# Decoding and splitting each weight tile once, with both parts kept in DRAM, in a fused attention and two-layer block on one core

## The chip, the cores and the metric

One core of a Trainium2 chip runs the whole program as one launch. The metric is the device time of that launch in microseconds. The kernel before takes 1089.96 us, the median of three runs (1089.48 to 1090.23).

## The reference

The inputs are float32 for attention and float64 for the weights of the two feed-forward layers (`moe_*`, `moe2_*`). Attention has 4 batches, 8 heads, 576 positions, head size 64; its bias comes from a small network on the relative position.

```python
scores = q @ k.T / 8 + bias(|i - j|, i)          # (4, 8, 576, 576)
attn   = exp(scores - rowmax) ; attn /= sum + 1e-9
x      = (attn @ v) as (2304, 512)               # tokens x model
h      = max(max(x @ w1, x @ w2), x @ w3)        # 512 -> 768
x      = h @ w_out                               # 768 -> 512
g      = elu(x @ w_in)                           # 512 -> 2048
out    = g @ w_out2                              # 2048 -> 512
```

## The kernel before

**Precision.** Each matrix product of the feed-forward layers is done with operands split into a high part `hi`, rounded to the matmul type fp32r, and a rest `lo = x - hi`. Three matmuls (hi·hi, hi·lo, lo·hi) replace one. The weights come as float64 bit patterns, so a tile of [128, 512] weights arrives as `raw`, [128, 512, 2] int32. The generator `decoder` (L350) turns it into float32 with five VectorE instructions (DVE: L358, L361, L363, L365, L368) and one ScalarE instruction (ACT: L360). Each `yield` ends a piece; `pump(k)` runs k pieces, so calls of `pump` spread the decoding over the program. Piece four also calls `fetch`, which issues the load of the tile after next.

**Weights.** There are 56 tiles: 18 for the first layer (`w1`: 6 column blocks m times 3 matrices w), 6 of its output matrix (`wo`), and 32 of the second layer (`wi` and `w3`, 16 each). The decoded float32 tiles stay in SBUF (`t10`, `T1`, `t2a`, `t2b`), except `wo`, which passes through DRAM (`scw`).

**Stages.** Everything is written out by hand (`manual_schedule`); engines run their instructions in program order.

1. The bias tables (L138 to L197) are computed and stored in DRAM.
2. Attention is a software pipeline of 80 steps, 5 for each of 16 head pairs and batches. `plan` holds (key, function) pairs; a step s puts its operations at keys s + `OFF`. At key s + 0.30 and 0.31 DVE computes the scores with the bias, at 0.32 comes one `pump` (59 of the 80 steps), then ACT evacuates the transposes of step s - 2 (`evac`, 0.36 to 0.39) and takes exponentials (`expo`, 0.38 and 0.40), with `norm` of step s - 1 on GpSimd (POOL) and DVE at 0.34 and 0.35. `lim` lets 9 tiles (3 `w1`, 6 `wo`) be decoded here.
3. The first layer goes over three token blocks th of 768 tokens. For each of the 18 tiles, `moe1_mm` runs 24 matmuls into one of 4 pairs of PSUM banks and `moe1_ev` takes the maximum (ACT for w = 0, DVE for w = 1, 2) and splits the result (ACT `hh`, POOL `hl`). `split_w1`, two tiles ahead, splits the float32 tile into hi and lo on POOL, and does so again for each th. In th = 0, `pump(3)` stands ahead of each evacuation: the other 15 `w1` tiles are decoded there. `moe1_out` multiplies by the output matrix (8 groups of 18 matmuls); for th = 0 and 1 it comes after the first column block of the next th.
4. The second layer goes over three token blocks blk and 16 blocks f: `moe2_g` (24 matmuls, then ELU and split) and `moe2_out` (18 matmuls of 512 columns). `split_w2` splits two tiles for each of the 48 (blk, f) on POOL. For blk = 0 `pump(5)` stands in each half of `moe2_g`, between two ACT instructions and ahead of the DVE instruction that frees the PSUM bank.

All DMAs are issued on SyncE (SP), in program order, each after the semaphores it waits for.

Of the kernel before, what the change touches and what calls it, by code (L numbers as in the profile page):

```python
# [10 lines left out]
F32 = mybir.dt.float32  # L11
# [15 lines left out]
NB = 384  # L27
# [21 lines left out]
def fused_kernel(ctx, tc, tkq, vv, lt, pk, wm1, wo1, win2, wo2, out):  # L49
# [3 lines left out]
    const = ctx.enter_context(tc.tile_pool(name="const", bufs=1))  # L53
    wpre = ctx.enter_context(tc.tile_pool(name="wpre", bufs=1))
    dram = ctx.enter_context(tc.tile_pool(name="dram", bufs=1, space=DRAM))

# [4 lines left out]

    scw = [dram.tile([128, 512], F32, name=f"scw{kk}") for kk in range(NM1)]
    scr = [dram.tile([128 if c < 4 else 64, H, S], F32, name=f"scr{c}") for c in range(5)]
# [9 lines left out]
    def lo_of(eng, dst, src, hi):  # L73
        e = nc.gpsimd if eng == "p" else nc.vector
        e.tensor_tensor(out=dst, in0=src, in1=hi.bitcast(F32), op=ALU.subtract)  # L75
# [173 lines left out]
    def trans0(s):  # L249
        n, c = steps[s]  # L250
        for k in range(4):
            nc.tensor.transpose(T0[:, 128 * k:128 * k + 128], E[s][:, 128 * k:128 * k + 128], ident)  # L252
        if c == 0:
            PT[n, 0] = [wpre.tile([128, 4, 256], F32, tag="big", name="p0", bufs=3) for _ in range(2)]
        elif c == 2:
            PT[n, 1] = [tp.tile([128, 4, 320], F32, tag=f"p{h}", name="p1", bufs=1) for h in range(2)]
        if c in (0, 2):
            PT[n, c // 2].append(tp.tile([128, 256], F32, tag="p3", name="p3", bufs=3))
        elif c == 4:
            PT[n, 1].append(tp.tile([64, 128], F32, tag="p4", name="p4", bufs=1))  # L260
# [65 lines left out]
    for m in range(NM1):  # L326
        DQ += [("w1", m, w) for w in range(3)]
        if m == 0:
            DQ += [("wo", kk, 0) for kk in range(NM1)]
    for f in range(NF):  # L330
        DQ += [("wi", f, 0), ("w3", f, 0)]
    RAW, TW = {}, {}
    n_raw = [0]
# [11 lines left out]

    dst_of = {}
    lim = [3 + NM1]

    def decoder():
        for i, key in enumerate(DQ):  # L350
            while i >= lim[0]:
                yield
            dst = dst_of[key[0]](key)
            t = dst.bitcast(I32)
# [13 lines left out]
            nc.vector.tensor_tensor(out=t, in0=t, in1=x, op=ALU.bitwise_or)  # L368
            TW[key] = dst
            yield  # L370
            if key[0] == "wo":
                yield
                nc.sync.dma_start(scw[key[1]], dst)
                yield

    def load_wo(kk):
        t = wpre.tile([128, 512], F32, tag="to", name="to", bufs=2)
        nc.sync.dma_start(t, scw[kk])
        return t

    def split_wo(kk, t):
        hi_of("a", WO["h"][:, kk, :], t)
        lo_of("p", WO["l"][:, kk, :], t, WO["h"][:, kk, :])

    dec = decoder()
    WO = {}

# [4 lines left out]
    def need(key):  # L392
        while key not in TW:
            next(dec)

    WS = {}

    def split_w1(th, m, w):
        hi, lo = wpre.tile([128, 2, 512], F32R, tag="big", name="whl", bufs=3).rearrange("p j n -> j p n")
        need(("w1", m, w))  # L400
        t = TW["w1", m, w]
        hi_of("p", hi, t)
        lo_of("p", lo, t, hi)
        WS[th, m, w] = (hi, lo)

    dst_of["w1"] = lambda key: t10[key[2]] if key[1] == 0 else T1[key[1] - 1][key[2]]
    dst_of["wo"] = lambda key: wpre.tile([128, 512], F32, tag="to", name="to", bufs=2)
    t10 = [wpre.tile([128, 512], F32, name=f"t10_{w}") for w in range(3)]

# [9 lines left out]
    def moe1_mm(th, m, w):  # L419
        hi, lo = WS.pop((th, m, w))  # L420
        ps = PS[th, m, w] = pair()
# [9 lines left out]
    def moe1_ev(th, m, w):  # L431
        ps = PS.pop((th, m, w))
        for blk in range(2):
            p = ps[blk][:, 0:NB]
            if th == 0 or (th == 1 and m == 0):
                pump(3)
            if w == 0:
# [48 lines left out]
    at(3.05, fetch)  # L486
    at(MOE_AT["s0"], split_w1, 0, 0, 0)
    at(MOE_AT["s1"], split_w1, 0, 0, 1)
    at(MOE_AT["mm"], moe1_mm, 0, 0, 0)
# [7 lines left out]

    lim[0] = 4 * NM1
    seq = [(blk, f) for blk in range(3) for f in range(NF)]

    W2 = {}

    def split_w2(nm, i):
        if i >= len(seq):
            return
        blk, f = seq[i]
        hi = ws.tile([128, 512], F32R, tag="h" + nm, name="h" + nm)
        lo = ws.tile([128, 512], F32R, tag="l" + nm, name="l" + nm)
        need((nm, f, 0))
        t = TW[nm, f, 0]  # L510
        hi_of("p", hi, t)
        lo_of("p", lo, t, hi)
        W2[nm, blk, f] = (hi, lo)


    with ExitStack() as m1:
        wop = m1.enter_context(tc.tile_pool(name="wop", bufs=1))
        hp_ = m1.enter_context(tc.tile_pool(name="hp", bufs=NM1 + 1))
        t1s = ExitStack()
        t1p = t1s.enter_context(tc.tile_pool(name="t1p", bufs=1, side="right"))  # L520

        WOH = WO["h"] = wop.tile([128, NM1, 512], F32R, name="woh")
        WOL = WO["l"] = wop.tile([128, NM1, 512], F32R, name="wol")
        T1 = [[t1p.tile([128, 512], F32, name=f"t1_{m}_{w}") for w in range(3)] for m in range(1, NM1)]
        def moe1_out(th):
            for m in range(NM2):
                ps = pair()
                ms = slice(128 * m, 128 * m + 128)
                for blk in range(2):
                    bs = slice(blk * NB, blk * NB + NB)  # L530
                    j = 0
                    for kk in range(NM1):
                        HH, HL = HT[th, kk]
                        for wt, xt in ((WOH, HH), (WOH, HL), (WOL, HH)):
                            mm(ps[blk][:, 0:NB], wt[:, kk, ms], xt[:, bs], start=(j == 0), stop=(j == 3 * NM1 - 1))  # L535
                            j += 1
                for blk in range(2):
# [4 lines left out]
                    nc.vector.tensor_tensor(out=xl, in0=p, in1=xh.bitcast(F32), op=ALU.subtract)  # L542
                    yield

        with tc.manual_schedule():
            order = [(th, m, w) for th in range(3) for m in range(NM1) for w in range(3)]
            for i, (th, m, w) in enumerate(order):
                if w == 0:
                    HT[th, m] = (hp_.tile([128, TB], F32R, tag="hh", name="hh"), hp_.tile([128, TB], F32R, tag="hl", name="hl"))
                if i + 2 < len(order):  # L550
                    split_w1(*order[i + 2])
                if th == 0 and m and w == 0:
                    wo_t = load_wo(m - 1), load_wo(m) if m == NM1 - 1 else None
                if th == 0 and m and w == 2:
                    split_wo(m - 1, wo_t[0])
                    if wo_t[1]:
                        split_wo(m, wo_t[1])
                if i:
                    moe1_mm(th, m, w)
                    moe1_ev(th, m, w)  # L560
                if m == 0 and w == 2 and th > 0:
                    for _ in moe1_out(th - 1):
                        pass
            t1s.close()
            t2a = ctx.enter_context(tc.tile_pool(name="t2a", bufs=1, side="right"))

            ws = ctx.enter_context(tc.tile_pool(name="ws", bufs=2, side="right"))
            dst_of["wi"] = dst_of["w3"] = lambda key: (t2a if key[1] < 3 else t2b).tile([128, 512], F32, name=f"t2_{key[0]}{key[1]}")
            lim[0] += 6
            for i, _ in enumerate(moe1_out(2)):  # L570
                pump(3)
                if i == 4:
                    split_w2("wi", 0)
                if i == 6:
                    split_w2("w3", 0)
                    split_w2("wi", 1)
            lim[0] = len(DQ)


    t2b = ctx.enter_context(tc.tile_pool(name="t2b", bufs=1))  # L580
    mp = ctx.enter_context(tc.tile_pool(name="mp2", bufs=2))
    GT = {}

    def moe2_g(blk, f):
        hi, lo = W2.pop(("wi", blk, f))
        GH = mp.tile([128, TB], F32R, tag="gh", name="gh")
        GL = mp.tile([128, TB], F32R, tag="gl", name="gl")
        GT[blk, f] = (GH, GL)
        for q in range(2):
# [9 lines left out]
            nc.scalar.activation(t, p, AF.Relu, scale=-1.0)  # L599
            if blk == 0 and f > 0:  # L600
                pump(5)
            nc.scalar.activation(t, t, AF.Exp, scale=-1.0)
# [5 lines left out]
    def moe2_out(blk, f, acc):  # L608
        hi, lo = W2.pop(("w3", blk, f))
        GH, GL = GT.pop((blk, f))  # L610
# [5 lines left out]
    with tc.manual_schedule():  # L616
        moe2_g(0, 0)
        for i, (blk, f) in enumerate(seq):
            split_w2("wi", i + 2)
            split_w2("w3", i + 1)  # L620
            if i + 1 < len(seq):
# [4 lines left out]
            if f == NF - 1:  # L626
                for t in range(6):
                    if t % 2 == 0:
                        o = wpre.tile([128, 2, 512], F32, tag="big", name="o_t", bufs=3)
                    r0 = blk * TB + 128 * t  # L630
# [70 lines left out]
```

## Time and profile before

| | us |
|---|---|
| median of three runs | 1089.96 |
| the profiled execution | 1089.01 |
| its span on the core | 1087.2 |
| PE (TensorE matmul) busy | 1036.8 |
| DVE busy | 564.3 |
| ACT busy | 489.7 |
| POOL busy | 534.0 |

Busy time is from the profiled execution. PE matmuls overlap, and their ends are modelled, so PE's busy time is an upper estimate; what limits a stage is read from the stage.

### The profile page before, as it was taken

What the parts mean: (1) busy time and instruction counts of PE and PEld (TensorE: products, weight loads), DVE (VectorE), ACT (ScalarE), POOL (GpSimd) and SP (SyncE); (2) the same over time, 40 slices, a digit from 0 to 9 for tenths busy, and PEclk for the clock granted to TensorE, in tenths of its full rate; (3) what the DMA queues carried; (4) which work ended last, traced back from release to release, by engine and by line L of the source; (5) the groups of instructions that cost most, each with busy time, mean ns of one, the idle gap of its engine ahead of it and who ended that gap; (6) DMA issues with size and microseconds to landing.
All of it is one profiled execution on the core that took longest, in us unless ns stands there. A gap on an engine that the chain in (4) does not pass through costs nothing.

```text
span 1087.2 us, 16728 instructions
## 1 busy us (share of the span) xinstructions
PE 1036.8 (95%) x6200; PEld 867.0 (80%) x6200; DVE 564.3 (52%) x1172; ACT 489.7 (45%) x1075; POOL 534.0 (49%) x541
## 2 busy tenths in 40 slices
PE   7999999999999869999999999878899999999998
PEld 4456666666668769999999998767789999999997
DVE  7977777777775991111111159999952111121111
ACT  8978788778872231111111124333334333343332
POOL 0022332323235557245605425767686677667663
PEclk9999999999999898999999999999999999999999
DMA  7733435243222330000000013333301000010001
GB/s 270 276 113 130 144 107 172 93 134 130 98 64 69 107 122 34 1 1 1 1 1 1 1 59 96 110 98 104 97 20 59 1 1 1 1 60 1 1 1 59
DMA packets 30674, 77.04 MB, mean 71 GB/s; under 512 B 5504, under 2 KB 6400, under 8 KB 30592
## 3 DMA queue, kind: packets, MB, share of 16 engines
q1 hardware_dynamic: 30592, 75.95, 21.1%
q8 instruction: 50, 0.82, 0.3%
q14 instruction: 32, 0.26, 0.1%
HBM read 59.03 MB, written 16.91 MB: 70 GB/s over the span
## 4 chain that ended last, share of the span: by engine, by line
PE 78%; DVE 16%; issue 3%; ACT 1%; POOL 1%; DMA 0%; DVEq 0%; SPq 0%; ACTq 0%; POOLq 0%
PE bk L596 13%; PE pb L614 9%; PE pb L428 8%; PE bk L428 8%; PE pb L219 7%; PE bk L294 7%; PE bk L614 4%; PE bk L252 4%; PE bk L535 3%; PE pb L535 3%; PE pb L181 2%; PE bk L264 2%; PE pbb L181 2%; DVE t_w L363 2%; DVE t_wi L361 2%
## 5 line engine op out<-in xcount | busy, mean ns | idle before, releaser
L245 POOL TENSOR_SCALAR e_t<-e_t,st_t 128x576 f32<-128x576 f32 x64 | 66.0, 1031 | 233.4 <-DVE st_t L239 215.2
L603 DVE SCALAR_TENSOR_TENSOR t_t<-t_t,bk 128x384 f32<-128x384 f32 x96 | 52.9, 551 | 233.1 <-POOL lw L75 169.0
L75 POOL TENSOR_TENSOR gl<-t_t,gh 128x384 fp32r<-128x384 f32 x96 | 100.8, 1050 | 125.7 <-ACT gh L69 125.3
L596 PE MATMUL bk<-xh,hwi 128*128 128x384 f32 x384 | 132.4, 345 | 21.4 <-DVE t_t L603 21.4
L228 DVE CUSTOM_DVE_ANT_0 e_t<-pb,b_t 128x576 f32<-128x576 f32 x144 | 104.0, 756 | 56.3 <-PE pb L219 35.8
L596 PE MATMUL bk<-xh,lwi 128*128 128x384 f32 x384 | 131.2, 342 | 0.0
L596 PE MATMUL bk<-xl,hwi 128*128 128x384 f32 x384 | 130.8, 341 | 0.0
L428 PE MATMUL pb<-xh,whl 128*128 128x384 f32 x448 | 119.5, 343 | 6.0 <-POOL whl L67 4.0
L69 ACT ACTIVATE p<-bk 128x512 f32<-128x512 f32 (+2 forms) x224 | 99.1, 473 | 53.9 <-PE bk L252 53.7
L428 PE MATMUL bk<-xh,whl 128*128 128x384 f32 x416 | 111.1, 343 | 8.5 <-POOL whl L67 7.0
L233 ACT ACTIVATE e_t<-e_t,st_t 128x576 f32<-128x576 f32 x144 | 111.8, 777 | 2.5 <-DVE st_t L228 2.5
L69 ACT ACTIVATE gh<-t_t 128x384 fp32r<-128x384 f32 x96 | 50.4, 525 | 138.0 <-DVE t_t L603 138.0
L599 ACT ACTIVATE t_t<-bk 128x384 f32<-128x384 f32 x96 | 46.1, 480 | 122.5 <-PE bk L596 122.5
L596 PEld LDWEIGHTS bk<-xh,hwi 128*128 128x128 f32 x384 | 73.4, 191 | 28.1 <-DVE t_t L603 25.6
L428 PEld LDWEIGHTS pb<-xh,whl 128*128 128x128 f32 x448 | 83.0, 192 | 7.4 <-POOL whl L67 4.3
L428 PEld LDWEIGHTS bk<-xh,whl 128*128 128x128 f32 x416 | 77.2, 193 | 9.9 <-POOL whl L67 7.6
L219 PE MATMUL pb<-kq_t 64*128 64x288 f32 x512 | 80.7, 429 | 1.3 <-DVE st_t L228 1.3
L294 PE MATMUL bk<-p,tv_t 128*64 128x320 f32 (+1 forms) x512 | 76.0, 418 | 0.5 <-ACT xf L315 0.5
L428 PE MATMUL pb<-xl,whl 128*128 128x384 f32 x224 | 76.4, 341 | 0.0
L614 PE MATMUL pb<-hw,gh 128*128 128x512 f32 x192 | 76.1, 397 | 0.0
L614 PE MATMUL pb<-lw,gh 128*128 128x512 f32 x192 | 76.0, 396 | 0.0
L69 ACT ACTIVATE hh<-a_t 128x384 fp32r<-128x384 f32 x36 | 18.5, 525 | 125.7 <-DVE a_t L441 125.6
(116 smaller groups left out, 2347.4 us busy)
## 6 DMA issues: line engine op xcount, KB each, us to landing
raw<-wo SPq DMA_DIRECT2D x22, 512.0 KB, 3.6
scr<-o_t SPq DMA_DIRECT2D x36, 288.0 KB, 3.6
kq_t<-tkq SPq DMA_DIRECT2D x16, 640.0 KB, 4.8
raw<-wm SPq DMA_DIRECT2D x18, 512.0 KB, 3.6
raw<-win SPq DMA_DIRECT2D x16, 512.0 KB, 3.6
tv_t<-vv SPq DMA_DIRECT2D x16, 384.0 KB, 3.4
b_t<-scr SPq DMA_DIRECT2D x16, 288.0 KB, 4.2
b_t<-scr SPq DMA_DIRECT2D x16, 256.0 KB, 4.0
```

The lines of the kernel that those rows point to most:

```text
L69: nc.scalar.activation(dst, src, AF.Copy)
L75: e.tensor_tensor(out=dst, in0=src, in1=hi.bitcast(F32), op=ALU.subtract)
L219: mm(PB[h][:, o], t[r, 640 + 128 * c:768 + 128 * c], t[r, k0:k0 + 288], start=True, stop=True)
L228: nc.vector.tensor_tensor_reduce(out=E[s][:, 576 * h:576 * h + 576], in0=PB[h][:, 224:800], in1=BT[n // 4, c, h], op0=ALU.add, op1=ALU.min ...
L233: nc.scalar.activation(e, e, AF.Exp, bias=st[:, h:h + 1], scale=-1.0, accum_out=st[:, 2 + h:3 + h])
L245: nc.gpsimd.tensor_scalar(e, e, r, 1.0, op0=ALU.mult, op1=ALU.mult)
L294: mm(XO[64 * h:64 * h + 64, 0:w], v[:, 128 * k + 64 * h:128 * k + 64 * h + 64], ps[h][:, k, :], start=(k == 0), stop=False, skip_group_che ...
L428: mm(ps[blk][:, 0:NB], wt[:, ks], xt[:, kk, t0:t0 + NB], start=(j == 0), stop=(j == 11))
L535: mm(ps[blk][:, 0:NB], wt[:, kk, ms], xt[:, bs], start=(j == 0), stop=(j == 3 * NM1 - 1))
L596: mm(p, wt[:, ks], xt[:, kk, t0:t0 + NB], start=(j == 0), stop=(j == 11))
L603: nc.vector.scalar_tensor_tensor(out=t, in0=t, scalar=-1.0, in1=p, op0=ALU.add, op1=ALU.max)
L614: mm(acc[t], g[:, ts], w, start=(f == 0 and j == 0), stop=(f == NF - 1 and j == 2))
```

## The change

All 56 tiles go through one stream, in the order `w1`, `wo`, then `wi` and `w3`. After the five decoding instructions the decoder itself splits the tile: ACT copies it into the high half of a new tile `sp2`, POOL subtracts into the low half, and one later piece issues a store of both halves (512 KB) to DRAM (`SCW`), one tile late. Each use loads both halves back into a ring of six buffers `wr`, four to five uses ahead. The splits on POOL at each use are gone, as are the resident float32 tiles. During attention 12 tiles may be decoded; in the first layer `pump(2)` stands ahead of each evacuation in all three token blocks, and `pump(3)` after each evacuation of `moe1_out`; the second layer has no `pump`.

```diff
+    wr = ctx.enter_context(tc.tile_pool(name="wr", bufs=6))
@@ DQ (order of tiles), lim
     for m in range(NM1):
         DQ += [("w1", m, w) for w in range(3)]
-        if m == 0:
-            DQ += [("wo", kk, 0) for kk in range(NM1)]
+    DQ += [("wo", kk, 0) for kk in range(NM1)]
-    lim = [3 + NM1]
+    lim = [12]
@@ decoder
-            dst = dst_of[key[0]](key)
+            dst = wpre.tile([128, 512], F32, tag="t", name="t_w", bufs=2)
...
             nc.vector.tensor_tensor(out=t, in0=t, in1=x, op=ALU.bitwise_or)
-            TW[key] = dst
+            sp2 = wpre.tile([128, 2, 512], F32R, tag="sp2", name="sp2", bufs=2)
+            hi_of("a", sp2[:, 0], dst)
+            lo_of("p", sp2[:, 1], dst, sp2[:, 0])
+            todo.append((key, sp2))
             yield
-            if key[0] == "wo":
-                yield
-                nc.sync.dma_start(scw[key[1]], dst)
-                yield
+            if len(todo) > 1:
+                store()
+    def store():
+        key, sp2 = todo.pop(0)
+        d = dram.tile([128, 2, 512], F32, name=f"scw_{key[0]}_{key[1]}_{key[2]}")
+        nc.sync.dma_start(d, sp2.bitcast(F32))
+        SCW[key] = d
+    def load_w(key):
+        need(key)
+        t = wr.tile([128, 2, 512], F32R, tag="w", name="w_t")
+        nc.sync.dma_start(t.bitcast(F32), SCW[key])
+        WS.append((key, t))
@@ moe1_ev
-            if th == 0 or (th == 1 and m == 0):
-                pump(3)
+            pump(2)
@@ moe1_out, after each evacuation
-                    yield
+                    pump(3)
@@ loop of the first layer
-                if i + 2 < len(order):
-                    split_w1(*order[i + 2])
+                load_w(nxt[i + 4])
...
+                if th == 0 and m == NM1 - 1:
+                    load_wo(2 * w)
+                    load_wo(2 * w + 1)
@@ moe2_g
-            if blk == 0 and f > 0:
-                pump(5)
@@ loop of the second layer
-            split_w2("wi", i + 2)
-            split_w2("w3", i + 1)
+            for key in load2[2 * i + 4:2 * i + 6]:
+                load_w(key)
```

## Rows read from the trace of the kernel before

**Rows 1.** Windows: stretch, length, busy (x instructions) of five engines, PEclk, DMA share, GB/s.
```profile
58.00:317.00 259.00, 258.10 (x1792) 162.68 (x1792) 198.79 (x610) 208.97 (x539) 76.74 (x92) 1.00 0.37 121
334.59:439.74 105.15, 91.19 (x482) 88.76 (x482) 71.73 (x94) 24.00 (x44) 66.30 (x60) 0.92 0.26 86
651.98:796.17 144.19, 122.77 (x582) 108.11 (x582) 138.91 (x169) 54.46 (x113) 95.70 (x79) 0.96 0.33 99
796.17:1082.40 286.23, 286.23 (x1434) 259.97 (x1434) 48.22 (x82) 106.84 (x216) 196.87 (x203) 0.99 0.04 13
```

**Rows 2.** Chain of work that ended last: start us, us, what.
```profile
334.59 4.38 PE pb L428 x24
...
439.74 6.26 PE pb L535 x36
...
464.72 4.16 PE pb L428 x24
...
717.30 1.45 DVE t_wi L361
...
727.87 1.45 DVE t_wi L361
...
845.74 4.19 PE bk L596 x24
...
854.05 4.19 PE bk L596 x24
```

**Rows 3.** Waits, 334 to 440 us and 652 to 796 us: total, times, longest.
```profile
PE bk L428 <- POOL whl L67: 7.0, 2, 5.4
...
PE bk L596 <- DVE t_t L603: 19.4, 12, 2.4
```

**Rows 4.** One line's instructions (ns min/median/max): two in attention, one 340 to 408.
```profile
L358 DVE TENSOR_SCALAR x_t<-raw x11: 418/425/449, 78.2 to 324.8; 128x512 int32<-128x512 int32 x11
...
L363 DVE SCALAR_TENSOR_TENSOR to<-raw,to x6: 689/702/707, 148.7 to 295.8; 128x512 int32<-128x512 int32 x6
...
L441 DVE TENSOR_TENSOR a_t<-bk,a_t x8: 545/549/553, 344.4 to 402.8; 128x384 f32<-128x384 f32 x8
```

**Rows 5.** Groups by line, 685.6 to 780.7 us: busy us, mean ns, idle before.
```profile
L361 DVE TENSOR_SCALAR t_wi<-raw 128x512 int32<-128x512 int32 x10 | 15.2, 1520 | 0.0
...
L603 DVE SCALAR_TENSOR_TENSOR t_t<-t_t,bk 128x384 f32<-128x384 f32 x18 | 9.8, 544 | 0.0
```

**Rows 6.** One line's instructions on POOL, 465 to 540 us.
```profile
L67 POOL TENSOR_SCALAR whl<-t x17: 618/619/627, 469.0 to 535.5; 128x512 fp32r<-128x512 f32 x17
...
L75 POOL TENSOR_TENSOR whl<-t,whl x17: 1289/1306/1308, 469.7 to 536.2; 128x512 fp32r<-128x512 f32 x17
L75 POOL TENSOR_TENSOR hl<-a_t,hh x11: 1013/1017/1020, 476.4 to 538.8; 128x384 fp32r<-128x384 f32 x11
```

**Rows 7.** Timeline of two attention steps: start us, us, engine, line, operation.
```profile
200.76 0.72 ACT L360 ACTIVATE x_t<-x_t,rebias 128x512 int32<-128x512 int32 x1
...
214.85 0.77 ACT L69 ACTIVATE p<-bk 128x512 f32<-128x512 f32 x2 [0.77 <-PE bk L252]
...
215.62 0.69 DVE L368 TENSOR_TENSOR to<-to,x_t 128x512 int32<-128x512 int32 x1
...
216.26 0.60 ACT L69 ACTIVATE p<-bk 128x512 f32<-128x512 f32 x1
...
216.78 0.97 POOL L245 TENSOR_SCALAR e_t<-e_t,st_t 128x576 f32<-128x576 f32 x1 [2.29 <-DVE st_t L239]
...
218.14 0.60 PE L264 MATMUL bk<-ident,e_t 128*128 128x128 f32 x4
```

**Rows 8.** Groups by line, whole span, ACT's copy of a 128x512 tile.
```profile
L69 ACT ACTIVATE woh<-to 128x512 fp32r<-128x512 f32 x6 | 3.6, 621 | 0.1
```

**Rows 9.** Windows, columns as in Rows 1: the busiest stretch of the DMA queue.
```profile
27.20:54.40 27.20, 27.20 (x333) 12.39 (x324) 27.20 (x65) 26.41 (x39) 0.00 (x0) 1.00 0.76 276
```

**Rows 10.** DMA issues: tile, count, KB each, median us to landing.
```profile
raw<-wm SPq DMA_DIRECT2D x18, 512.0 KB, 3.6
...
out<-o_t SPq DMA_DIRECT2D x15, 256.0 KB, 2.5
scw<-to SPq DMA_DIRECT2D x6, 256.0 KB, 4.3
```

More of the change, by code (lines that the diff above doesn't have):

```diff
@@ L60, in fused_kernel @@
     nc.vector.memset(rebias, -896.0 * 2.0 ** 23)
-    scw = [dram.tile([128, 512], F32, name=f"scw{kk}") for kk in range(NM1)]
     scr = [dram.tile([128 if c < 4 else 64, H, S], F32, name=f"scr{c}") for c in range(5)]
@@ L253, in trans0 @@
         if c == 0:
-            PT[n, 0] = [wpre.tile([128, 4, 256], F32, tag="big", name="p0", bufs=3) for _ in range(2)]
+            PT[n, 0] = [tp.tile([128, 4, 256], F32, tag="pa", name="p0", bufs=3) for _ in range(2)]
         elif c == 2:
@@ L327, in fused_kernel @@
         DQ += [("w1", m, w) for w in range(3)]
-        if m == 0:
-            DQ += [("wo", kk, 0) for kk in range(NM1)]
+    DQ += [("wo", kk, 0) for kk in range(NM1)]
     for f in range(NF):
         DQ += [("wi", f, 0), ("w3", f, 0)]
-    RAW, TW = {}, {}
+    RAW = {}
     n_raw = [0]
@@ L344, in fetch @@
         RAW[key] = r
-    dst_of = {}
-    lim = [3 + NM1]
+    lim = [12]
+    SCW = {}
     def decoder():
@@ L368, in decoder @@
             nc.vector.tensor_tensor(out=t, in0=t, in1=x, op=ALU.bitwise_or)
-            TW[key] = dst
+            sp2 = wpre.tile([128, 2, 512], F32R, tag="sp2", name="sp2", bufs=2)
+            hi_of("a", sp2[:, 0], dst)
+            lo_of("p", sp2[:, 1], dst, sp2[:, 0])
+            todo.append((key, sp2))
             yield
-            if key[0] == "wo":
-                yield
-                nc.sync.dma_start(scw[key[1]], dst)
-                yield
-    def load_wo(kk):
[L377 to L383, printed above, removed]
+            if len(todo) > 1:
+                store()
+        while todo:
+            store()
+    todo = []
+    def store():
[3 more added lines that the diff above has]
+        SCW[key] = d
+    def load_wo(kk):
+        need(("wo", kk, 0))
+        nc.sync.dma_start(WO[:, kk].bitcast(F32), SCW["wo", kk, 0])
     dec = decoder()
-    WO = {}
     def pump(k=1):
@@ L392, in need, with take_w @@
     def need(key):
[L393 to L408, printed above, removed]
+        while key not in SCW:
+            if all(k != key for k, _ in todo):
+                next(dec)
+            else:
+                store()
+    WS = []
+    def load_w(key):
[3 more added lines that the diff above has]
+        WS.append((key, t))
+    def take_w(key):
+        k, t = WS.pop(0)
+        assert k == key
+        return t[:, 0], t[:, 1]
     TB = 2 * NB
@@ L419, in moe1_mm @@
     def moe1_mm(th, m, w):
-        hi, lo = WS.pop((th, m, w))
+        hi, lo = take_w(("w1", m, w))
         ps = PS[th, m, w] = pair()
@@ L486, in fused_kernel @@
     at(3.05, fetch)
-    at(MOE_AT["s0"], split_w1, 0, 0, 0)
-    at(MOE_AT["s1"], split_w1, 0, 0, 1)
+    for i in range(4):
+        at(MOE_AT["s0"], load_w, ("w1", i // 3, i % 3))
     at(MOE_AT["mm"], moe1_mm, 0, 0, 0)
@@ L495, in fused_kernel @@
     att.close()
-    lim[0] = 4 * NM1
     seq = [(blk, f) for blk in range(3) for f in range(NF)]
[L501 to L513, printed above, removed]
+    load2 = [("wi", 0, 0)]
+    for i, (blk, f) in enumerate(seq):
+        load2 += [("wi", s[1], 0) for s in seq[i + 1:i + 2]] + [("w3", f, 0)]
+    lim[0] = len(DQ)
     with ExitStack() as m1:
@@ L518, in fused_kernel @@
         hp_ = m1.enter_context(tc.tile_pool(name="hp", bufs=NM1 + 1))
[L519 to L524, printed above, removed]
+        WO = wop.tile([128, NM1, 2, 512], F32R, name="wo_t")
         def moe1_out(th):
@@ L533, in moe1_out @@
                         HH, HL = HT[th, kk]
-                        for wt, xt in ((WOH, HH), (WOH, HL), (WOL, HH)):
-                            mm(ps[blk][:, 0:NB], wt[:, kk, ms], xt[:, bs], start=(j == 0), stop=(j == 3 * NM1 - 1))
+                        for wt, xt in ((0, HH), (0, HL), (1, HH)):
+                            mm(ps[blk][:, 0:NB], WO[:, kk, wt, ms], xt[:, bs], start=(j == 0), stop=(j == 3 * NM1 - 1))
                             j += 1
@@ L542, in moe1_out @@
                     nc.vector.tensor_tensor(out=xl, in0=p, in1=xh.bitcast(F32), op=ALU.subtract)
-                    yield
+                    pump(3)
         with tc.manual_schedule():
             order = [(th, m, w) for th in range(3) for m in range(NM1) for w in range(3)]
+            nxt = [("w1", m, w) for th, m, w in order] + load2[:4]
             for i, (th, m, w) in enumerate(order):
@@ L549, in fused_kernel @@
                     HT[th, m] = (hp_.tile([128, TB], F32R, tag="hh", name="hh"), hp_.tile([128, TB], F32R, tag="hl", name="hl"))
-                if i + 2 < len(order):
-                    split_w1(*order[i + 2])
[L552 to L557, printed above, removed]
+                load_w(nxt[i + 4])
                 if i:
@@ L560, in fused_kernel @@
                     moe1_ev(th, m, w)
+                if th == 0 and m == NM1 - 1:
+                    load_wo(2 * w)
+                    load_wo(2 * w + 1)
                 if m == 0 and w == 2 and th > 0:
[L562 to L580, printed above, removed]
+                    moe1_out(th - 1)
+            moe1_out(2)
     mp = ctx.enter_context(tc.tile_pool(name="mp2", bufs=2))
@@ L584, in moe2_g @@
     def moe2_g(blk, f):
-        hi, lo = W2.pop(("wi", blk, f))
+        hi, lo = take_w(("wi", f, 0))
         GH = mp.tile([128, TB], F32R, tag="gh", name="gh")
@@ L608, in moe2_out @@
     def moe2_out(blk, f, acc):
-        hi, lo = W2.pop(("w3", blk, f))
+        hi, lo = take_w(("w3", f, 0))
         GH, GL = GT.pop((blk, f))
@@ L628, in fused_kernel @@
                     if t % 2 == 0:
-                        o = wpre.tile([128, 2, 512], F32, tag="big", name="o_t", bufs=3)
+                        o = mp.tile([128, 2, 512], F32, tag="o", name="o_t", bufs=3)
                     r0 = blk * TB + 128 * t
```

## The prediction

> **What bounds the kernel now.** First the windows by stage. In attention PE is busy 258.10 of 259.00 us, DVE 198.79 and ACT 208.97 [rows 1]: PE sets the pace, and the other two have about a fifth of the time free. In the first token block of the first layer the picture turns: PE 91.19 of 105.15 us. In the first token block of the second layer PE has 122.77 of 144.19 and DVE 138.91; in the rest of that layer PE is never idle [rows 1].
>
> Next the chain of waits, for the length of one unit of work. A step of the first layer (24 matmuls) is 4.16 us and one `moe1_out` is 464.72 - 439.74 = 24.98 us. A step of the second layer, where PE is full, is 854.05 - 845.74 = 8.31 us; in its first token block it is 727.87 - 717.30 = 10.57 us, and the chain there runs through DVE's decoding instructions [rows 2].
>
> From these the two losses:
> - First layer: from 334.59 to 439.74 lie 20 steps. 105.15 - 20 x 4.16 = 21.9 us lost. The other two token blocks show none.
> - Second layer: from 651.98 to 1082.40 lie 48 steps. 430.4 - 48 x 8.31 = 31.5 us lost, all in the first token block.
>
> Last the waits: PE waits for the split on POOL in the one, for the DVE instruction that frees the bank in the other [rows 3]. That DVE instruction stands behind `pump(5)`, so DVE's decoding is the cause. Why is it so slow? A decoding instruction with one source takes 0.425 us alone, one with two 0.69 to 0.70 us, so a tile costs 2 x 0.425 + 3 x 0.69 = 2.92 us [rows 4, 7]. In the first token block of the second layer the same 0.425 us instruction takes 1.52 us [rows 5], since POOL splits two tiles per step at that time. DVE instructions that read PSUM keep their length (0.549 and 0.544 us) [rows 4, 5]. So decoding and POOL's work mostly take turns. Per step of 10.57 us they are, alone: DVE 2 x 2.92 + 2 x 0.544 = 6.93, POOL 2 x (0.619 + 1.306) + 2 x 1.017 = 5.88 [rows 5, 6]. Together 12.81; the step took 0.825 of that.
>
> The Trainium skill ("SBUF — State Buffer", section "SBUF: two separate sides") has a rule for this: VectorE and GpSimd share a pair of SBUF ports under an exclusive lock, and the one that comes second waits for the whole instruction. The trace agrees, with 1.52 against 0.425 us. Strictly by it decoding and POOL's work never overlap at all; what that would give is the second rival.
>
> **The change part by part.** The sum starts from the profiled execution, 1089.0 us (span 1087.2 and 1.8 around it), 1.0 us under the median.
>
> *Second layer.* No decoding and no split of weights is left: DVE has two instructions of 0.55 us per step, POOL two of 1.02. PE is left with 8.31 us per step. The loads, two of 512 KB per 8.31 us (126 GB/s), are issued over a step ahead and land in about 3.6 us [rows 10]. Gain 31.5 us. If the loads came late it would show here, but the queue moves 276 GB/s elsewhere [rows 9].
>
> *First layer.* Two `pump(2)` per step and five pieces per tile make 0.8 tiles a step, now through all three token blocks until the stream ends. After attention 44 tiles are left, so 221 pieces: 17 steps (68), 3 (12), a `moe1_out` (24), 15 (60), 3 (12), a `moe1_out` (24), and 5 more steps. That is 43 steps and two `moe1_out`, 43 x 4.16 + 2 x 24.98 = 228.8 us of PE. Per step DVE has 0.8 x 2.92 + 4/3 x 0.549 = 3.07 us, POOL 0.8 x 1.306 + 2/3 x 1.017 = 1.72 (one subtraction per tile is left). Sum 4.79; by the 0.825 above 3.96 us, under 4.16. In `moe1_out` it is 24.8 before overlap against 24.98. PE waits only when it is four pairs of banks ahead, so bursts are smoothed. PE stays the bound: gain the whole 21.9 us, but with only 0.2 us of cover per step.
>
> ACT per step: 0.8 x (0.72 + 0.62) and 4/3 evacuations of about 0.5, some 1.8 of 4.16 us [rows 7, 8]. Its copy waits for DVE and for the store of two tiles before; behind it wait the evacuations, with four banks' pairs of room. On SP each `fetch` waits for DVE's fourth piece, and behind it stand stores and loads; a load is issued some four steps, 17 us, before its use. Both cost nothing so.
>
> *The DMA queue in that stretch.* 44 tiles x 1.05 MB (raw in, halves out) + 43 loads and 6 of `wo` at 0.52 MB = 71.8 MB in 228.8 us, 314 GB/s. No stretch of before shows that. From below: 276 GB/s at a share of 0.76 [rows 9] makes 363 at full use, so 198 us, no cost. From above: raw tiles of this very shape at 99 GB/s and 0.33 [rows 1] make 300, so 239 us, +10.5. The nearest row is the second, but its queue is nearly empty; I take the middle, +5 us. (The Trainium skill, "DMA: Bandwidth & Descriptors", section "Where 436 GB/s comes from", gives about 358 GB/s between HBM and a core; by that estimate 201 us and no cost, so a forecast 5 us lower. No run here shows it yet.)
>
> *Attention.* 12 tiles instead of 9, and every `pump` now has a piece: 14 more DVE pieces of 0.425 to 0.70 us, hidden in DVE's free fifth. The splits are not hidden. ACT's copy is emitted in the same piece as the last DVE instruction, at 0.32, ahead of ACT's evacuations. In the step shown, that instruction ends at 215.62 + 0.69 = 216.31, while ACT would start its evacuations at 214.85 [rows 7]. With a copy of 0.62 us [rows 8] they start at 216.93, 2.08 us late; the last of them ends at 218.94 instead of 216.86. POOL subtracts until 218.24, and `norm`, which ended at 217.75, ends at 219.21. PE's transposes that need both started at 218.14 [rows 7]: 1.07 us late, and PE, the bound, doesn't get it back. Nine of the twelve splits meet such a step; for three the step before has no second head, and I take 0.3 us. 9 x 1.07 + 3 x 0.3 = 11 us. From below 0: the exponent's 0.72 us in the same place of ACT's queue [rows 7] hurts nobody, as its input is a step old. From above the whole delay, 12 x 2.08 = 25 us. A gain is excluded, as PE is full.
>
> Sum: 1089.0 - 31.5 - 21.9 + 11 + 5 = 1052 us.
>
> **Rivals.**
> 1. *All is hidden.* PE's slack takes up the late copies, and the queue keeps pace: 1089.0 - 53.4 = 1036 us. For it: ACT and DVE a fifth free. Against: both wait in order, and PE has 0.9 us free of 259.
> 2. *DVE and POOL take turns strictly* in the first layer: 4.79 us a step, 0.63 x 43 = 27 us: 1089.0 - 53.4 + 11 + 27 = 1074 us. For it: 1.52 against 0.425 us. Against: the 0.825 of before, and PSUM instructions that are not slowed.
> 3. *Attention pays the full delay*: 12 x 2.08 = 25 us instead of 11, so 1066 us. For it: ACT needs about three steps to catch up. Against: the banks in question are needed a step later.
> 4. *Slower: the stores clog the one DMA queue.* The small store of before, 256 KB, landed in 4.3 us, an output of the same size in 2.5 [rows 10]. If each of the 44 stores in the first layer holds the queue 1.8 us longer, the 239 us become 318, 89 more than PE needs: 1089.0 - 53.4 + 11 + 89 = 1136 us. It decides from (228.8 + 42.4 - 239) / 44 = 0.73 us per store. For it: that row. Against: 276 GB/s, stores among them, at a share of 0.76.
>
> That the change doesn't do what it says would show as decoding in bursts where a load finds its tile not stored. By the count above the stream stays two tiles or more ahead of first use (24 decoded when the first `wo` is loaded), so I give this no chance of its own.
>
> **How the numbers follow.** Forecast 0.56, with a range of its own from 1040 to 1064; rivals 0.13, 0.13, 0.10 and 0.08. The time is the forecast's, 1052. The range reaches from under rival 1 to over rival 2, 1030 to 1082, and leaves out rival 4 and some misjudged size. A difference under 0.2% (2 us) can't be told from none. Only rival 4, and a sum of several bad ends, is slower: 0.10; within 0.2%: 0.02; faster 0.88.
>
> **What would show it.** Steps of 8.31 us from the start of the second layer, and PE without idle time there (right). The first layer's steps at 4.16 us in all token blocks; if it is 4.8 with decoding instructions of over 1 us, rival 2. The decoding stretch with a DMA share near 1, and DVE waiting for `raw`: queue. In attention a step some 1.1 us longer at each split, with ACT's copy waiting for DVE. The forecast is wrong at its root if the first layer's second and third token blocks, which were free of stalls, lose more than the 53 us that is regained.

## The result, and the profile after

The changed kernel takes 1053.95 us (median of four runs, 1051.88 to 1055.14); the kernel before took 1089.72 us in the same job. The ratio is 0.9673, 95% interval [0.9653, 0.9693]: 3.3% faster. The forecast was 1052 us, the range 1030 to 1082. The profile is of the execution of 1055.14 us.

The page of the profile after: span, busy time of the engines, then busy tenths in 40 slices of the span, for DVE the digit row, for DMA the share and GB/s.

```profile
span 1053.4 us, 16952 instructions
...
PE 1022.5 (97%) x6200; PEld 858.2 (81%) x6200; DVE 531.5 (50%) x1172; ACT 517.4 (49%) x1125; POOL 299.9 (28%) x291
...
DVE  7977778777775688578897611111121111211111
...
DMA  7742635436234588969987940434336343363341
GB/s 266 274 141 65 217 90 200 143 111 207 98 120 161 175 299 296 345 202 324 339 292 199 352 129 9 131 121 136 124 114 206 120 130 131 107 212 122 124 136 61
```

DVE's decoding now fills the first layer up to the 23rd slice (its last instruction starts at 594 us) and is gone from the second layer. POOL's time falls from 534.0 to 299.9 us. The DMA queue moves about 290 GB/s in the first layer while tiles are decoded (255 over the whole layer) and 129 in the second.

The windows by stage (columns as in [rows 1]; attention, first layer, second layer):

```profile
58.00:316.00 258.00, 248.45 (x1710) 155.61 (x1710) 197.49 (x595) 204.80 (x528) 87.06 (x99) 1.00 0.42 138
348.91:652.10 303.19, 297.68 (x1702) 296.49 (x1703) 209.58 (x313) 94.20 (x180) 107.55 (x82) 0.99 0.74 255
652.10:1048.30 396.20, 396.20 (x2016) 361.43 (x2015) 60.31 (x107) 148.66 (x300) 97.47 (x96) 1.00 0.39 129
```

In the second layer PE is never idle. In attention it is now idle: 9.6 of 258 us, where it had 0.9 of 259 [rows 1]. To place the change exactly, take two landmarks of the chain of waits that both kernels have: the last products of attention (`bk L294 x16`) and the last half of the third `moe1_out` (x72). Of the kernel after:

```profile
330.84 4.93 DMA w_t<-scw_w
...
335.82 6.00 PE pb L435 x24
...
345.70 2.32 PE bk L294 x16
...
639.62 12.48 PE pb L524 x72
...
862.65 4.16 PE bk L567 x24
...
870.90 4.16 PE bk L567 x24
...
1046.94 1.37 PE bk L583 x6
```

Of the kernel before, the rows that answer to them:

```profile
331.33 2.37 PE bk L294 x16
...
639.48 12.50 PE pb L535 x72
...
1081.07 1.39 PE bk L614 x6
```

| stretch | before | after | difference |
|---|---|---|---|
| to the last products of attention | 331.33 | 345.70 | +14.4 |
| from there to the last `moe1_out` | 308.15 | 293.92 | -14.2 |
| from there to the last matmuls | 441.59 | 407.32 | -34.3 |

The sum, -34.1 us, is the difference of the spans (1087.2 to 1053.4) to 0.3 us.

Who waits for whom in the kernel after (total us, times, longest):

```profile
ACT sp L69 <- DMA scw_wi<-sp: 36.8, 10, 7.0
...
PE bk L268 <- POOL e_t L245: 8.5, 9, 1.0
...
DVE x_t L358 <- DMA raw<-wo: 6.5, 3, 4.9
...
PE pb L435 <- DMA w_t<-scw_w: 3.9, 2, 3.1
PE pb L524 <- DMA wo_t<-scw_wo: 3.6, 2, 2.0
PE bk L435 <- DMA w_t<-scw_w: 1.1, 1, 1.1
```

Nine waits of about 0.9 us for POOL's `norm`, all in attention; one of 3.1 us for the very first load of a split tile; and 5.5 us in the first layer (3.6, 1.1 and the other 0.8 of L435), for loads that land late. ACT's long wait, for the store that frees the tile it copies into, is not among them: every wait of PE's matmuls in the first layer is for a load. One split in attention, in the timeline:

```profile
116.41 0.69 DVE L368 TENSOR_TENSOR t_w<-t_w,x_t 128x512 int32<-128x512 int32 x1
...
117.13 0.63 ACT L69 ACTIVATE sp<-t_w 128x512 fp32r<-128x512 f32 x1 [2.25 <-DVE t_w L368]
...
117.84 1.27 POOL L75 TENSOR_TENSOR sp<-t_w,sp 128x512 fp32r<-128x512 f32 x1 [2.55 <-ACT sp L69]
...
119.09 0.75 POOL L245 TENSOR_SCALAR e_t<-e_t,st_t 128x576 f32<-128x576 f32 x1
...
119.89 0.33 PE L268 MATMUL bk<-ident,e_t 128*128 128x128 f32 x1 [0.91 <-POOL e_t L245]
```

ACT stands idle 2.25 us before the copy, until DVE's last decoding instruction is done; POOL's subtraction follows, `norm` after it, and PE's transpose waits 0.91 us.

### The profile page after: what moved, and what is told of

It is laid out like the page before. It is cut to its first block, busy times and chain, and to the rows that moved or that the text cites. A ratio compares the mean times of both kernels' runs of the same rounds, so it can differ in the third digit from the quotient of the medians.

```text
span 1053.4 us, 16952 instructions
## 1 busy us (share of the span) xinstructions
PE 1022.5 (97%) x6200; PEld 858.2 (81%) x6200; DVE 531.5 (50%) x1172; ACT 517.4 (49%) x1125; POOL 299.9 (28%) x291
## 4 chain that ended last, share of the span: by engine, by line
PE 79%; DVE 7%; DMA 5%; issue 4%; POOL 3%; ACT 2%; SPq 0%; POOLq 0%; ACTq 0%; DVEq 0%
PE bk L567 19%; PE pb L583 12%; PE pb L435 8%; PE bk L435 7%; PE bk L583 6%; PE pb L219 5%; PE bk L294 5%; PE pb L181 3%; PE bk L524 2%; PE pb L524 2%; PE bk L252 2%; PE pbb L181 2%; POOL e_t L245 2%; DVE e_t L228 2%; DVE t_w L365 2%
## 5 line engine op out<-in xcount | busy, mean ns | idle before, releaser
L567 PE MATMUL bk<-xh,w_t 128*128 128x384 f32 x768 | 203.4, 336 | 0.0
L567 PEld LDWEIGHTS bk<-xh,w_t 128*128 128x128 f32 x768 | 139.3, 188 | 1.9
L567 PE MATMUL bk<-xl,w_t 128*128 128x384 f32 x384 | 128.9, 336 | 0.0
L75 POOL TENSOR_TENSOR sp<-t_w,sp 128x512 fp32r<-128x512 f32 x56 | 78.7, 1405 | 172.7 <-ACT sp L69 172.7
L435 PE MATMUL pb<-xh,w_t 128*128 128x384 f32 x448 | 118.8, 340 | 3.9 <-DMA w_t<-scw_w 3.9
L69 ACT ACTIVATE sp<-t_w 128x512 fp32r<-128x512 f32 x56 | 35.5, 634 | 174.8 <-DVE t_w L368 62.5
L583 PE MATMUL pb<-w_t,gh 128*128 128x512 f32 x384 | 118.6, 390 | 0.0
L435 PE MATMUL bk<-xh,w_t 128*128 128x384 f32 x416 | 108.5, 336 | 1.1 <-DMA w_t<-scw_w 1.1
L435 PEld LDWEIGHTS pb<-xh,w_t 128*128 128x128 f32 x448 | 82.2, 190 | 4.5 <-DMA w_t<-scw_w 3.3
L219 PE MATMUL pb<-kq_t 64*128 64x288 f32 x512 | 80.7, 429 | 1.3 <-DVE st_t L228 1.3
L583 PEld LDWEIGHTS pb<-w_t,gh 128*128 128x128 f32 x384 | 71.4, 188 | 11.8
L435 PEld LDWEIGHTS bk<-xh,w_t 128*128 128x128 f32 x416 | 75.4, 188 | 1.4 <-DVE a_t L447 1.4
L294 PE MATMUL bk<-p,tv_t 128*64 128x320 f32 (+1 forms) x512 | 76.0, 418 | 0.0
L435 PE MATMUL pb<-xl,w_t 128*128 128x384 f32 x224 | 75.8, 339 | 0.0
```

The costliest lines, as they stand in the source:

```text
L69: nc.scalar.activation(dst, src, AF.Copy)
L219: mm(PB[h][:, o], t[r, 640 + 128 * c:768 + 128 * c], t[r, k0:k0 + 288], start=True, stop=True)
L294: mm(XO[64 * h:64 * h + 64, 0:w], v[:, 128 * k + 64 * h:128 * k + 64 * h + 64], ps[h][:, k, :], start=(k == 0), stop=False, skip_group_che ...
L435: mm(ps[blk][:, 0:NB], wt[:, ks], xt[:, kk, t0:t0 + NB], start=(j == 0), stop=(j == 11))
L567: mm(p, wt[:, ks], xt[:, kk, t0:t0 + NB], start=(j == 0), stop=(j == 11))
L583: mm(acc[t], g[:, ts], w, start=(f == 0 and j == 0), stop=(f == NF - 1 and j == 2))
```

## The experiments

Each is an edit of the changed kernel; the diffs are shortened, and remarks behind `#` are added to them. Ratios are to the kernel before in the same job; the changed kernel has 0.9673, and 0.9683 when repeated (below).

**The split one piece later.**

```diff
-            hi_of("a", sp2[:, 0], dst)
-            lo_of("p", sp2[:, 1], dst, sp2[:, 0])
-            todo.append((key, sp2))
+            late.append((key, sp2, dst))
             yield
+            split()     # both instructions and todo.append, after the next tile's first piece
```

> The split of a tile (ACT copy, POOL subtraction) is moved one piece later, behind the next tile's first decoding instruction, so its input is a step old when its turn comes. Theory (the copy stands in ACT's queue in the same step in which DVE makes its input; evacuations and norm wait behind it): the about 1 us per split goes from attention, some 10 us in all, 1044 us (1042 to 1047). Rival (the subtraction of 1.3 us ahead of norm on POOL is what holds PE, wherever its input comes from): 1051 to 1054.

Measured: 1039.2 us, ratio 0.9555 [0.954, 0.957], some 13 us less than the change. The landmark in its chain:

```profile
325.17 5.79 PE pb L441 x24
...
334.84 2.32 PE bk L294 x16
...
622.16 12.48 PE pb L530 x72
```

Attention ends at 334.84 instead of 345.70: 10.9 us are back, 10.2 of them from the stalls at splits and 0.7 at the first load, whose wait is shorter here. PE has no wait for `norm` any more. The rival (the subtraction harms wherever its input comes from) falls. The time is some 3 us under the 1042 to 1047 expected; the first layer, which takes 287.32 us here, varies by more than that (below).

**Only POOL's subtraction later.**

```diff
             hi_of("a", sp2[:, 0], dst)
-            lo_of("p", sp2[:, 1], dst, sp2[:, 0])
-            todo.append((key, sp2))
+            late.append((key, sp2, dst))
             yield
+            split()     # lo_of and todo.append, after the next tile's first piece
```

> ACT's copy stays, only POOL's subtraction moves one piece later. Theory (two chains of nearly equal length, over ACT 0.80 us and over POOL 1.07 us late): PE still waits for the evacuations, only some 0.2 to 0.3 us per split come back, 1050 to 1052 us. Rival (PE is held by POOL alone): nearly all comes back, 1044 to 1046.

Measured: 1051.27 us, ratio 0.9649 [0.9628, 0.967]; the interval overlaps the change's. The trace decides: attention ends at 342.67, 3.0 us earlier, and PE waits in another place.

```profile
PE bk L264 <- ACT p L69: 5.0, 9, 0.6
...
342.67 2.32 PE bk L294 x16
```

Nine waits of 0.6 us for ACT's evacuations have taken the place of nine of 0.9 for POOL. Two chains of nearly equal length, as the theory had it: mending one of them gives little more than the difference.

**The first loads two attention steps earlier**.

```diff
-        at(MOE_AT["s0"], load_w, ("w1", i // 3, i % 3))
+        at(77.388, load_w, ("w1", i // 3, i % 3))
```

> The first four loads of split tiles are issued two attention steps earlier. Theory (PE waits for the first load at the start of the first layer, 3.1 us, and then runs its first 24 matmuls at the low clock, 6.0 instead of 4.2 us): about 3.6 us less, 1050 us. Rival (the drain of attention ends no earlier, other work hides it): 1054 us.

Measured: 1045.39 us, ratio 0.9608 [0.9592, 0.9624], 7 us less. In its chain the first 24 matmuls take 4.17 instead of 6.00 us, and attention ends 5.2 us earlier:

```profile
332.42 4.17 PE pb L435 x24
...
340.48 2.32 PE bk L294 x16
```

The wait of 3.1 us and the 1.8 us of slow matmuls make 4.9; the theory holds, its price was too low, and some 2 us of the difference lie in the first layer, which varies (below).

**No raw loads from the 13th tile on.** The two last raw tiles are decoded again and again; the weights, and so the output, are those of other tiles.

```diff
+        if n_raw[0] > 12:
+            RAW[key] = kept[n_raw[0] % 2]
+            return
-        r = wpre.tile([128, 512, 2], I32, tag="raw", name="raw", bufs=2)
+        r = kept[n_raw[0] % 2] = wpre.tile([128, 512, 2], I32, tag="raw", name="raw", bufs=2)
```

> From the 13th tile on no raw tile is loaded; the two last ones are decoded again (so the weights are wrong), with all DVE, ACT and POOL work kept. 23 of the 72 MB in the first layer go. Theory (the 7.7 us that the first layer loses are the DMA queue: loads of the output weights and of the tiles landing late): 5 to 7 us less, 1047 to 1049 us. Rival (decoding and POOL's work taking turns are the bound): under 2 us, 1052 to 1054.

Measured: 1043.16 us, ratio 0.958 [0.9565, 0.9594].

```profile
342.97 2.32 PE bk L294 x16
...
628.10 12.48 PE pb L528 x72
```

From landmark to landmark 285.13 us instead of 293.92: the first layer loses nothing that a trace shows, with DVE's, ACT's and POOL's work unchanged, and PE waits for no load there. The rival falls. The first load no longer stands behind a raw one, so its wait and the slow matmuls behind it are gone too, 4.9 us; attention ends only 2.7 us earlier because this execution had lost 2.2 us early on, before the edit changes anything: its granted clock was 0.54 from 60 to 65 us and 0.78 from 65 to 70, against 1.00 in the kernel after. So the raw loads are the cause. How they do it stays open in part: without them transfers land sooner (split tiles in 4.7 us instead of 7.7, stores in 2.8 to 3.5 instead of 6.5 to 8.7), but SP's waits for DVE ahead of each `fetch` are gone as well. A crowded queue and loads issued late are not told apart.

**Putting the second layer's work back.** In `pool_back` POOL splits every tile again at each use; in `dve_back` ten decoding pieces per step stand at their old place in the first token block; `both_back` has both in that block. Nobody reads the results.

```diff
     hi, lo = take_w(("wi", f, 0))     # and the same in moe2_out
+    a = mp.tile([128, 512], F32R, tag="da", name="d_a", bufs=1)
+    b = mp.tile([128, 512], F32R, tag="db", name="d_b", bufs=1)
+    hi_of("p", a, hi.bitcast(F32))
+    lo_of("p", b, hi.bitcast(F32), a)
```

> In the second layer POOL splits again, for every use of a tile, into scratch that nobody reads; nothing else is changed. Theory (splits on POOL cost PE nothing where DVE has nothing to decode, as in the later token blocks of the kernel before): 1054 us, at most the 2.6 us by which a step of the second layer is now shorter than it was (8.26 against 8.31), 1054 to 1057. Rival (POOL's work at each use was a good part of the loss): over 1060.

Measured: 1051.0 us, ratio 0.9673 [0.9649, 0.9697]. No cost.

```diff
     nc.scalar.activation(t, p, AF.Relu, scale=-1.0)     # in moe2_g, for each half
+    if blk == 0 and f > 0:
+        for _ in range(5):
+            next(red)     # pieces of the decoding, on one raw tile loaded once
```

> In the first token block of the second layer ten decoding pieces per step are put back at their old place, on one raw tile and without its loads, their result unused; no split on POOL. Theory (decoding is slow only where POOL splits beside it: DVE 6.93 + POOL 2.03 = 8.96 us alone, times 0.825 is 7.4, under 8.26 per step): 1054 to 1058 us. Rival (decoding ahead of the instruction that frees the bank is enough): 10.5 us per step, about 1085 to 1090.

Measured: 1052.86 us, ratio 0.9686 [0.9666, 0.9705]. No cost that can be told.

```diff
+    if blk == 0:
+        hi_of("p", a, hi.bitcast(F32))
+        lo_of("p", b, hi.bitcast(F32), a)
...
+    if blk == 0 and f > 0:
+        for _ in range(5):
+            next(red)
```

> Both of these in the first token block of the second layer: ten decoding pieces and two splits on POOL per step. Theory (the two take turns; 12.81 us of work per step at 0.825): the loss of the kernel before comes back, 15 steps x 2.3 us = 34, so 1082 to 1090 us. Rival (the loss had to do with the raw loads or with waiting for freshly decoded tiles): under 1065.

Measured: 1085.06 us, ratio 0.998 [0.9965, 0.9996]. The window 661 to 780 us, first with DVE's pieces alone, then with both (columns as in [rows 1]):

```profile
661.00:780.00 119.00, 119.00 (x598) 106.39 (x597) 113.46 (x170) 54.62 (x114) 28.54 (x29) 1.00 0.37 124
```

```profile
661.00:780.00 119.00, 100.28 (x473) 88.28 (x472) 115.12 (x137) 43.99 (x92) 79.50 (x67) 0.96 0.30 98
```

The chain of the last one gives the step:

```profile
694.21 0.35 DVE t_w L565
...
704.78 0.34 DVE t_w L565
```

10.57 us, to the hundredth the step of the kernel before [rows 2]. Either half alone is hidden, both together cost 33 us: PE falls from 119.00 to 100.28 of 119.00. With its pieces alone DVE is nearly as busy (113.46 of 119.00) as with both (115.12), so its busy share does not show whether it is the bound. Both runs are of the second layer; that the first layer before the change lost its time in the same way is read from its waits [rows 3], and no run tests it.

**Three pieces per step from the second token block on.**

```diff
         for blk in range(2):
-            pump(2)
+            pump(2 if th == 0 or blk == 0 else 1)
```

> From the second token block of the first layer on, three pieces per step instead of four, so the stream ends in the last column block and moves about 260 instead of 314 GB/s there. Theory (the queue's late loads cost 2 us in that part): 1050 to 1053 us. Rival (the loss sits in the first token block and its output product, where nothing changes): 1054.

Measured: 1050.82 us, ratio 0.9657 [0.9642, 0.9672]. Between landmarks 289.18 us. Inconclusive: the change itself varies more from one execution to the next, as the following run shows.

**The changed kernel again, and the three edits together.**

> The changed kernel as it is, beside the next one on the same chip: 1051 to 1055 us. Its first layer lost 7.7 us in the first profile; if that is the state of a crowded queue rather than a fixed wait, this profile shows another loss there, between 3 and 9 us.

Measured: 1053.7 us, ratio 0.9683 [0.9656, 0.9711]. Its profile, span 1047.4, has

```profile
344.94 2.32 PE bk L294 x16
...
633.66 12.48 PE pb L524 x72
```

so 288.72 us between landmarks, against 293.92 before. The first layer's loss, counted from the 285.13 of the run without raw loads, is 3.6 us in one execution and 8.8 in another. `pool_back` and `dve_back` leave the first layer as it is and lie between, at 4.6 and 5.0 us (289.74 and 290.12). Edits that cost or give 2 us there can't be told by one profile.

`best` has the edits of `late_split`, `early_load` and `slow_pump`.

> Later split, earlier first loads and three pieces per step from the second token block on, together. Theory (three separate losses: 10.9 us of stalls in attention, some 5 us at the first load, 2 us in the queue): 1031 to 1035 us. Rival (they overlap: what is regained in attention is lost at the first load, since the drain sets its end): 1036 to 1040.

Measured: 1033.75 us (1031.63 to 1034.31), ratio 0.9498 [0.9478, 0.9518], 20 us less than the change and the fastest of all.

```profile
331.06 2.32 PE bk L294 x16
...
616.19 12.48 PE pb L530 x72
```

Attention ends where it did before the change (331.33), and the first layer takes 285.13 us. Its window shows PE busy throughout:

```profile
334.27:641.14 306.87, 306.87 (x1764) 306.01 (x1765) 209.02 (x319) 102.31 (x194) 110.44 (x86) 1.00 0.74 256
```

The losses add up; the rival falls. Which of the three edits frees the first layer is not shown: alone they leave 2.2 us (`late_split`), 6.7 (`early_load`) and 4.1 (`slow_pump`) of its loss in their profiles.

## Why the prediction was right, point by point

- *What bounds the kernel.* Right. The second layer's first token block lost its time to decoding and splitting side by side. `dve_back` and `both_back` show it: 6.93 + 2.03 us of work is hidden behind a step of PE, 12.81 us gives 10.57 again. That confirms the factor 0.825 for the mix of work from which it was taken, and for no other. The Trainium skill's rule of the exclusive lock ("SBUF — State Buffer", section "SBUF: two separate sides") agrees in kind. Taken strictly, without overlap, it would have made 11.7 us of that step: the 12.81 without the two DVE instructions that read PSUM, which kept their length. The prediction's "since POOL splits two tiles per step" is too narrow: in `dve_back`, where POOL only makes the ELU's low part (two subtractions of 1.02 us a step), one decoding instruction of each tile takes 1.495 us all the same. At 700.38 us, for one, it starts 0.07 us behind a subtraction on POOL and ends 0.55 us after it, nearly a full turn; the other four keep their length.

```profile
L567 DVE SCALAR_TENSOR_TENSOR t_w<-r_r,t_w 128x512 int32<-128x512 int32 x23 | 34.4, 1495 | 0.8
```

- *Second layer, -31.5.* Measured -34.3. The mechanism is as told. The rest is the step itself: 870.90 - 862.65 = 8.25 us instead of 8.31, times 48 is 2.9 us. `pool_back` has the 8.25 us step as well, so POOL's splits were not the reason; nor was the clock, granted at 1.00 in that stretch before and after. It stays open.
- *First layer, -21.9 + 5.* Measured -14.2 in one profile and -19.4 in another (308.15 - 288.72). The loss of 5 us to the queue was chosen between 0 and 10.5; 3.6 to 8.8 were measured. The middle fits, but it was a choice between two bounds and came from no mechanism. `no_raw` shows that the raw loads cause the loss. Its shape was not foreseen: not a rate that is too low throughout, but a few late landings. In the stretch 349 to 523 us of the kernel after (issues, KB each, median us to landing):

```profile
w_t<-scw_w SPq DMA_DIRECT2D x32, 512.0 KB, 7.7
...
raw<-wo SPq DMA_DIRECT2D x16, 512.0 KB, 6.3
```

  A load lands in 7.7 us instead of 3.5 in the second layer. PE then waits, longest at the output weights (3.6 us), which SP could not load until the last of them had been stored. The waits make 5.5 of the 8.8 us. After the longest the clock falls as well, to a mean of 0.96 in 42 us, some 1.7 us more, as the next row shows; the rest is not told apart.

```profile
433.00:475.00 42.00, 38.38 (x212) 37.76 (x211) 29.31 (x50) 14.85 (x29) 12.86 (x11) 0.96 0.74 244
```

- *DVE and POOL in the first layer.* Rival 2 (strict turns, 4.79 us a step) did not come. PE has 8.32 us for two steps wherever no load is late, and decoding with two sources took 0.93 to 0.95 us on the mean there, between 0.69 alone and the 1.49 that was seen in the second layer (L365 is one of them):

```profile
L365 DVE SCALAR_TENSOR_TENSOR t_w<-raw,t_w 128x512 int32<-128x512 int32 x30 | 28.6, 954 | 0.7
```

  But the rival was priced too high: without the 0.73 us of instructions that read PSUM, which the prediction itself says are not slowed, strict turns make 4.06 us, under PE's 4.16. So the first layer can't tell strict turns from partial overlap.

- *Attention, +11.* Right, in mechanism and size. (9 x 1.07 + 3 x 0.3 is 10.5; the sum took 11.) In the kernel before and in the kernel after, the last product of q and k in L219 starts at 314.3 and at 325.0 us, 10.7 us later:

```profile
L219 PE MATMUL pb<-kq_t x504: 402/403/507, 58.1 to 314.3; 64*128 64x288 f32 x168
```

```profile
L219 PE MATMUL pb<-kq_t x504: 402/403/507, 58.1 to 325.0; 64*128 64x288 f32 x168
```

  The delay comes in nine jumps of 1.1 to 1.3 us (1.07 predicted) and two of 0.14; a listed wait of 0.9 us is shorter than the delay it stands for, since matmuls overlap. That ACT is late by nearly as much as POOL is shown by `late_lo`.
- *What was missed.* "Both cost nothing so" was said of SP's waits, for loads issued 17 us ahead. It does not hold for the first load: that stands behind `fetch` in SP's queue, is issued at 330.84 and lands at 335.77, while PE is ready for it at 332.7. The wait of 3.1 us and the 1.8 us of slow matmuls make 4.9; with the 10.7 above, less 1.1 us of other waits that the end of attention had before, attention came to +14.4 instead of +11. Nor does it hold for the output weights in the first layer.
- *The total.* Against the profiled execution (1055.1 us) the terms were off by +3.4 (attention), +2.7 (first layer) and -2.8 us (second layer), together +3.3; the median lies 1.2 us under that execution. That the forecast hit to 2 us is in part luck: a cost that was left out and a gain that was not foreseen nearly cancel.
- *Rival 4* (stores clog the queue) falls: the first layer's loss is 4 to 9 us, not 89. *Rivals 1 and 3* fall with 10.7 us of stalls.

## What to carry to other kernels

Count the work of engines that slow each other where it runs side by side: each of two pieces of work can be hidden behind the bound and both together not, so removing either may give the whole gain. Put an instruction into an in-order queue one turn after its input is made; a copy of 0.6 us that waits 2 us for its input delays all that stands behind it. Where two such chains are of nearly equal length, mending one shows only the other. When a prefetch is added, check the first one by itself: its distance is that of the place where it is issued, not of the steady state.

## What the runs showed of the hardware that was not expected

- The DMA queue's rate in 40 slices of the stretch 349 to 523 us (4.35 us each) of the kernel after:

```profile
GB/s 0 113 354 320 380 204 264 371 410 346 87 305 271 410 396 138 325 347 419 243 275 403 398 116 232 222 213 121 273 261 402 412 202 335 360 402 333 284 230 403
```

  In single slices it reaches 419 GB/s with loads and stores mixed. That is over the 358 GB/s that the Trainium skill gives as the limit between HBM and one core, half of what two cores share ("DMA: Bandwidth & Descriptors", section "Where 436 GB/s comes from"); this program runs one core. The mean, 290 at a DMA share of 0.83, would be 349 at a full share, inside the 300 to 363 that were worked out from before. By this estimate the 71.8 MB need 206 us of the queue, less than PE's 228.8: the rate alone would have cost nothing.
- After PE had stood idle for 3.1 us at the first load, its next 24 matmuls took 6.00 us, at a granted clock of 0.72 on the mean, so for a part of them at 1.2 instead of 2.4 GHz; without the wait they took 4.17 at 1.00:

```profile
335.82:341.82 6.00, 6.00 (x26) 5.75 (x28) 0.00 (x0) 0.00 (x0) 0.00 (x0) 0.72 1.02 357
```

  A wait of PE cost more than half its length again.
